# An early x tile in two loads, one z1 tile in other PSUM banks, and x tiles 2 to 4 taken transposed from DRAM

## The chip, the cores and the metric

One core of one Trainium2 chip runs the whole kernel. A core has TensorE (PE in the views; its weight loads are PEld), VectorE (DVE), ScalarE (ACT), GpSimd (POOL) and SyncE (SP), 16 DMA engines that serve queues issued from SP, ACT and POOL, an on-chip SBUF of 128 partitions, and eight PSUM banks that PE writes. The metric is the time of one execution in device microseconds, as the median of several runs.

## The reference, cut to what matters

All is float32: a sequence of 2048 rows of 512 features, 32 heads of 16.

```python
xn = layernorm(x)                                    # per row
# branch A: linear attention with a learned feature map
q, k, v = split(xn @ wqkv)                           # 32 heads of 16
pq, pk  = q @ w_phi, k @ w_phi                       # per head
phi(p)  = concat(softmax(p), softmax(-p))
o = phi(pq) (phi(pk)^T v) / (phi(pq) . sum(phi(pk)) + 1e-6)
# branch B: gated MLP that mixes along the sequence
z  = gelu(xn @ w_in);  z1, z2 = halves of z          # 688 columns each
g  = w_sp @ layernorm(z2) + b_sp                     # 2048 x 2048 mixing matrix
out = x + o @ wo + (z1 * g) @ w_out
```

## The kernel before

A float32 product is made of three products of rounded halves: each operand is split into a high part (`round_h`, mostly on ACT) and a rest (`rest_l`, mostly on DVE), and `mm3` (lines 51 to 55) adds high·high, high·low and low·high in PSUM. The 2048 rows are 16 tiles of 128 rows (`NT`). PE needs each x tile transposed, features on the partitions, and split: that is `xT[s]`.

The layernorm is never applied as such. A tile is centred (its row means taken away), and the reciprocal deviation `r_x[:, s]` is put on where a product leaves PSUM, as the `scale` of the activation. `stats` (line 251) makes mean and variance on DVE, `rstd_of` (line 84) two small POOL operations.

There are two ways from x in DRAM to `xT[s]`:

- **By PE.** The tile is loaded with rows on the partitions (`load_x`), centred on DVE (`centered_on_dve`, tiles 0, 1 and 3) or on ACT (`center`, tiles 2 and 4), and turned by four PE transposes into a PSUM bank (`transposed`, line 290). `split_x` (line 244) then reads the bank. Tiles 0 to 4 go this way (`XT0 = 5`).
- **By DMA.** `fetch_T` (line 265) loads a block of `x_t`, a copy of x that is transposed in 128 x 128 pieces ahead of the kernel, into a `raw` buffer (two of them). The same tile also comes with rows on the partitions, for its statistics alone. `mean_out` (line 271) puts the negated means into a padded 128 x 32 tile, turns that with a DVE transpose of 32 x 32 blocks, and stores the row to DRAM (`nm_d`) from SP's queue. `mean_in` (line 281) is an accumulating transfer on POOL's queue: it reads that row for all 128 partitions and adds it to `raw`. `split_x` then reads `raw` from SBUF. Tiles 5 to 15 go this way.

The first stage (`p0`, from line 175) runs so. The loads are issued in one written order (lines 340 to 351): x tile 0, the value weights (on ACT's and SP's queues in turn), x tile 1, the feature map `bd`, the key weights, x 2, the query weights, x 3, the first half of `w_in` (`w1r`, four pieces of 344 KB), x 4 and 5, the bias. Then a block (line 373 on) whose order is written out: `keep` makes everything issued later on an engine stay behind the instruction that it is given. It holds warm-up matmuls, tile 0's centring, transposes and value projection, tile 1, the folding of the feature map into the key weights (`fold`, 128 small matmuls, then `folded` which rounds the result), the value projection of tile 1, the key projection of tiles 0 and 1, and the folding of the query weights in two halves (the first half's last rounding on ACT is `q_half`).

After that comes the loop over the 16 tiles (line 427). Per tile: the key softmax pair on DVE and ACT (`softmax_k`), `split_x` of tile s+2, loads for tiles s+4 and s+5, `normalise` with an accumulation of 512 KB into `zacc` on POOL's queue, the value projection of tile s+1, mean transfers for tile s+4, query projections, z1 products (`z1_raw`: a zero to one tile per step, in PSUM pool `za`), and every second step `run`, which holds the PE order of transposes and the key-value products (`add_kv`). The four roundings of `w1r` on ACT and their rests on POOL (1.68 us each, to `w1_hl`) are traced in step 1 and stay behind `q_half`.

Within what the written order leaves open, a planner chooses each engine's order at compile time from its own cost estimates; `tc.issue_after(i)` puts a block's instructions behind `i` on `i`'s engine. An engine runs its own list in that fixed order and waits where an input or a buffer is not ready.

PSUM in this stage: `kv_ps` two banks, `za` two, `p0ps` four, of which the projections and the transposes take tag `mm`. When the stage ends, `p0ps` is given back, and `zb` (`zbp`, one tile of two banks) and `psk` (two) take its place. The last five z1 tiles (`LAG = 5`, s = 11 to 15) alternate: odd ones in `zbp`, even ones in `za` (line 578).

Later stages (z2, the mixing with `w_sp` in seven products per pair of tiles, the gate, the output) aren't touched.

Of the kernel before, what the change touches and what calls it, by code (L numbers as in the profile page):

```python
# [10 lines left out]
F32 = mybir.dt.float32  # L11
# [16 lines left out]
EPS_LN = 1e-5  # L28
EPS_DEN = 1e-6
XB = 3  # L30
XT0 = 5
NP = NT // 2
HP, QP = P // 2, P // 4
SQ = 32
# [3 lines left out]
def mixer(ctx: ExitStack, tc: tile.TileContext, x, x_t, wv, wqkT, phi_bd, wo, w_in, wst, b_r, w_out, out):  # L38
# [45 lines left out]
    def rstd_of(mv, r, stats=None):  # L84
        if stats is not None:
            dve.bn_aggr(mv, stats)
        pool.tensor_scalar_add(mv[:, 1:2], mv[:, 1:2], EPS_LN)
        pool.tensor_tensor(r, mv[:, 1:2], mhalf, op=ALU.pow)
# [83 lines left out]
    with ExitStack() as p0:  # L172
# [67 lines left out]
        def fetch(s):  # L240
            if s < NT:
                xt[s] = load_x(s)

        def split_x(src):
            t = xz.tile([P, 2, FH], F32R, tag="xz", name="xT")
            xT.append(t)
            src = src.rearrange("p a b -> p (a b)")
            return round_h(act, t[:, 0, :D], src), rest_l(t[:, 1, :D], src, t[:, 0, :D])
# [3 lines left out]
            dve.bn_stats(st6, xt[s])  # L252
            return dve.bn_aggr(mv_x[:, s], st6).ins

        def center(s):
            nm = wk.tile([P, 1], F32, tag="nm", name="nm")
            pool.tensor_scalar_mul(nm, mv_x[:, s, 0:1], -1.0)
            rstd_of(mv_x[:, s], r_x[:, s:s + 1])
            return act.activation(xt[s], xt[s], AF.Identity, bias=nm).ins

        raws = {}
        nm_pad = wk.tile([P, SQ], F32, tag="pad", bufs=1, name="nm_pad")
        pool.memset(nm_pad, 0.0)
# [1 line left out]
        def fetch_T(s):  # L265
            if s < NT:
                raws[s] = wk.tile([P, ND * P], F32, tag="raw", name="raw")
                sp.dma_start(raws[s], x_t[s].rearrange("p a b -> p (a b)"))
                fetch(s + 1)

        def mean_out(s):
            stats(s)
            xt.pop(s)
            dve.tensor_scalar_mul(nm_pad[:, :1], mv_x[:, s, 0:1], -1.0)
            row = wk.tile([P, SQ], F32, tag="nmT", bufs=1, name="nmT")
            dve.transpose(row, nm_pad)
            rstd_of(mv_x[:, s], r_x[:, s:s + 1])
            sp.dma_start(nm_d[s].rearrange("c (b t) -> b c t", t=SQ),
                         row.rearrange("(b k) t -> b k t", k=SQ)[:, 0].unsqueeze(1).to_broadcast([P // SQ, ND, SQ]))

        def mean_in(s):
            pool.dma_start(raws[s], nm_d[s:s + 1].rearrange("a c t -> a (c t)").to_broadcast([P, ND * P]), accum_op=ALU.add)

        def centered_on_dve(s):
            stats(s)
# [4 lines left out]
        def transposed(s):  # L290
            xs = xt.pop(s)
            pt = ps.tile([P, ND, P], F32, tag="mm", name="pt")
            for c in range(ND):
                ins = pe.transpose(pt[:, c], xs[:, c * P:(c + 1) * P], ident).ins
            return pt, ins
# [24 lines left out]
                                start=s == 0 and m < 4, stop=s == NT - 1, skip_group_check=True).ins  # L320
            return ins

        def run(tiles, feats):

            with ExitStack() as order:
                for i in ahead_of_run:
                    order.enter_context(tc.issue_after(i))
                ahead_of_run.clear()
                pts = []
                for t in tiles:  # L330
                    pt, i = transposed(t)
                    pts.append(pt)
                    order.enter_context(tc.issue_after(i))
                for t, e in feats:
                    i = add_kv(t, e)
            for pt in pts:
                split_x(pt)
            return i

        fetch(0)  # L340
        wvr = load_rows(wv, queues=(act, sp))
        fetch(1)
        sp.dma_start(bd, phi_bd.rearrange("p g f -> p (g f)"))
# [2 lines left out]
        wqT = load_rows(wqkT[:D])  # L346
        fetch(3)
        w1r = load_rows(w_in[:, :FH], FH)
        fetch(4)
        fetch(5)  # L350
        sp.dma_start(bias, b_r)


        def keep(**ins):
            for i in ins.values():
                queue.enter_context(tc.issue_after(i))
# [16 lines left out]
        with ExitStack() as queue:  # L373
            warm = wk.tile([P, 2 * P], F32, tag="v", bufs=4, name="warm")
            keep(dve=dve.memset(warm, 1.0).ins)
            tbl = wk.tile([P, 1], F32, tag="nm", name="tbl")
            keep(act=act.activation(tbl, mhalf, AF.Identity, bias=mhalf).ins)
            warm_up(4)
            keep(dve=centered_on_dve(0))
            split_v(0)  # L380
            split_v(1)
            pt, i = transposed(0)
            keep(pe=i)
            warm_up(1)
            split_x_kept(pt)
            split_v(2)
            split_v(3)
            keep(dve=centered_on_dve(1))
            keep(dve=stats(2))
            i, j = proj_v(0, True)  # L390
            keep(pe=i, act=j)
            pt, i = transposed(1)
            keep(pe=i)
            split_x_kept(pt)
            keep(act=center(2))
            accs = [fold_banks(pl, n) for n, pl in enumerate((za, kv_ps_p))]
            for g in range(NG):
                keep(pe=fold(wkT, g, accs))
            folded(1, accs, keep)
            kvps = kv_ps_p.tile([P, D], F32, tag="z", name="kvps")  # L400
            kv_acc = kvps[:, :NG * HP].rearrange("p (g b) -> p g b", b=HP)
            pt, i = transposed(2)
            keep(pe=i)
            split_x_kept(pt)
            keep(dve=centered_on_dve(3))
            keep(pe=proj_v(1)[0])
            p = proj(0, wqk_h[:, 1], wqk_l[:, 1], True)
            keep(pe=proj.last)
            pt, i = transposed(3)
            keep(pe=i)  # L410
            split_x(pt)
            ek = softmax_k(0, p)
            for k in range(2):
                accs = [fold_banks(za, k)]
                for g in range(NG):
                    i = fold(wqT, g, accs)
                q_parts = {}
                folded(0, accs, q_parts.update)
                if k == 0:
                    q_half = q_parts["act"]  # L420
                    keep(pe=i)
                    p1 = proj(1, wqk_h[:, 1], wqk_l[:, 1])
                    keep(pe=proj.last)
        n1 = nq = 0
        feats, shifted = [], softmax_pair.shifted
        behind = ExitStack()
        for s in range(NT):
            er = ek if s == 0 else softmax_k(s, p1 if s == 1 else proj(s, wqk_h[:, 1], wqk_l[:, 1]))
            ahead_of_run.append(proj.last)
            if XT0 <= s + 2 < NT:  # L430
                with tc.issue_after(softmax_pair.exp):
                    split_x(raws.pop(s + 2).rearrange("p (a b) -> p a b", b=P))
            if s:
                fetch_T(s + 4)
            feats.append((s, normalise(er)))
            if 0 < s < NT - 1:
                ahead_of_run.append(proj_v(s + 1)[0])
            if s == 1:
                with tc.issue_after(shifted):
                    stats(4)  # L440
                with tc.issue_after(q_half):
                    center(4)
            if 0 < s < NT - 4:
                with tc.issue_after(shifted):
                    mean_out(s + 4)
                with tc.issue_after(normalise.last):
                    mean_in(s + 4)
                shifted = softmax_pair.shifted
            while nq < (s - 2) * NT // (NT - 3):
                proj_q(nq)  # L450
                ahead_of_run.append(proj.last)
                nq += 1
            if s == 1:
                with tc.issue_after(q_half):
                    for c in range(ND):
                        round_h(act, w1_hl[0][:, c], w1r[c])
                        rest_l(w1_hl[1][:, c], w1r[c], w1_hl[0][:, c], pool)
            while n1 < (s + 1) * (NT - LAG) // (NT - 1):
                z1_raw(wk, za, n1, 2)
                n1 += 1  # L460
            if s and s % 2 == 0:
                last = run([t for t in (s + 2,) if t < XT0], feats[:-1])
                behind.close()
                behind.enter_context(tc.issue_after(last))
                del feats[:-1]
# [79 lines left out]
    with ExitStack() as p1:  # L545
# [27 lines left out]
        with ExitStack() as p1a:  # L573
            ta = p1a.enter_context(left("tmp1a", 1))
            for j in range(2):
                load_win(w2[j], 2 + j, ta)
            for s in range(NT - LAG, NT):
                z1_raw(tmp1, (za, zbp)[s % 2], s, 2)
                if s == NT - LAG + 1:
                    make_zb()  # L580
            make_kvT()
            raw[0], raw[1] = load_a(0), load_a(1)
            A[0] = prep_a(0, raw.pop(0))
# [406 lines left out]
```

## Time and profile before

| what | us |
|---|---|
| median of 3 runs (637.16 to 637.48) | 637.43 |
| the profiled execution | 638.0 |
| its span, first to last instruction | 636.3 |
| PE busy in it | 629.2 |
| DVE busy | 509.7 |
| ACT busy | 267.2 |
| POOL busy | 113.5 |

The granted TensorE clock is 0.999 of full over the span. The page gives busy time per engine over the whole span, so an engine that is nearly always busy in one stage can look half idle. The views used below are the page (whole span), waits (who waited for whom: total, times, longest), the timeline (start, duration, engine, line, operation, `x` the number merged, and in brackets the idle time before it with what ended it), groups by line or by tile, DMA issues with the time to landing, and busy time by window. A timeline row with a `q` behind the engine (`SPq`) is the issuing of a transfer, not the transfer.

### The profile page before, as it was taken

What the parts mean: (1) busy time and instruction counts of PE and PEld (TensorE: products, weight loads), DVE (VectorE), ACT (ScalarE), POOL (GpSimd) and SP (SyncE); (2) the same over time, 40 slices, a digit from 0 to 9 for tenths busy, and PEclk for the clock granted to TensorE, in tenths of its full rate; (3) what the DMA queues carried; (4) which work ended last, traced back from release to release, by engine and by line L of the source; (5) the groups of instructions that cost most, each with busy time, mean ns of one, the idle gap of its engine ahead of it and who ended that gap; (6) DMA issues with size and microseconds to landing.
All of it is one profiled execution on the core that took longest, in us unless ns stands there. A gap on an engine that the chain in (4) does not pass through costs nothing.

```text
span 636.3 us, 11626 instructions
## 1 busy us (share of the span) xinstructions
PE 629.2 (99%) x4467; PEld 571.2 (90%) x4467; DVE 509.7 (80%) x941; ACT 267.2 (42%) x446; POOL 113.5 (18%) x195
## 2 busy tenths in 40 slices
PE   8999999999999999999999999999999999999997
PEld 6888888888887999999999999999999887888886
DVE  5979989998898578889987868678695698989521
ACT  5623333332432448887443434434353433323330
POOL 4542231322101014341010010100101200001000
PEclk9999999999999999999999999999999999999999
DMA  9467676656644941002464352543548877675620
GB/s 329 142 165 162 192 183 148 192 142 155 182 136 112 309 141 66 2 1 73 140 191 126 117 170 87 176 131 113 179 151 265 274 269 271 246 266 218 210 67 35
DMA packets 41908, 103.95 MB, mean 163 GB/s; under 512 B 5404, under 2 KB 6940, under 8 KB 41852
## 3 DMA queue, kind: packets, MB, share of 16 engines
q1 hardware_dynamic: 28524, 58.37, 28.5%
q0 software_dynamic: 10736, 38.67, 21.2%
q10 hardware_dynamic: 2592, 6.16, 2.5%
q8 instruction: 35, 0.57, 0.4%
q14 instruction: 21, 0.17, 0.1%
HBM read 62.01 MB, written 26.50 MB: 139 GB/s over the span
## 4 chain that ended last, share of the span: by engine, by line
PE 94%; DVE 4%; issue 1%; DMA 1%; ACT 0%; POOL 0%
PE g L55 11%; PE g L54 11%; PE g L53 11%; PE proj L53 6%; PE proj L55 6%; PE proj L54 6%; PE zps L53 6%; PE zps L55 6%; PE zps L54 6%; PE pout L53 6%; PE pout L54 5%; PE pout L55 5%; PE ptq L863 1%; PE po L877 1%; PE pout L895 1%; PE kvps L319 1%
## 5 line engine op out<-in xcount | busy, mean ns | idle before, releaser
L54 PE MATMUL g<-B,A 128*128 128x344 f32 x448 | 143.3, 320 | 0.0
L55 PE MATMUL g<-B,A 128*128 128x344 f32 x448 | 143.3, 320 | 0.0
L53 PE MATMUL g<-B,A 128*128 128x344 f32 x448 | 143.3, 320 | 0.0
L54 PEld LDWEIGHTS g<-B,A 128*128 128x128 f32 x448 | 84.2, 188 | 0.0
L55 PEld LDWEIGHTS g<-B,A 128*128 128x128 f32 x448 | 84.2, 188 | 0.0
L53 PEld LDWEIGHTS g<-B,A 128*128 128x128 f32 x448 | 84.2, 188 | 0.0
L49 DVE TENSOR_TENSOR A<-S,A 128x512 fp32r<-128x512 f32 x64 | 43.7, 688 | 29.9 <-ACT A L45 29.1
L45 ACT ACTIVATE A<-S 128x512 fp32r<-128x512 f32 x64 | 40.1, 631 | 59.5 <-PE g L55 35.8
L113 ACT ACTIVATE e<-e,r_x 128x1024 f32<-128x1024 f32 x32 | 36.8, 1149 | 49.9 <-DVE e L112 48.0
L45 ACT ACTIVATE A<-wf 128x512 fp32r<-128x512 f32 x64 | 33.4, 522 | 39.8 <-PE g L55 34.5
L53 PE MATMUL proj<-wqk_h,xT 128*128 128x512 f32 x124 | 49.6, 400 | 0.0
L55 PE MATMUL proj<-wqk_h,xT 128*128 128x512 f32 x124 | 48.8, 394 | 0.0
L54 PE MATMUL proj<-wqk_l,xT 128*128 128x512 f32 x124 | 48.7, 393 | 0.0
L115 DVE TENSOR_REDUCE sm<-e 128x64 f32<-128x1024 f32 x32 | 38.6, 1211 | 8.8 <-ACT e L113 8.6
L53 PE MATMUL zps<-w_h,xT 128*128 128x344 f32 x128 | 41.8, 327 | 1.3 <-DVE e L112 0.9
L49 DVE TENSOR_TENSOR A<-wf,A 128x512 fp32r<-128x512 f32 x64 | 35.4, 553 | 8.4 <-ACT A L45 8.0
L55 PE MATMUL zps<-w_h,xT 128*128 128x344 f32 x128 | 40.9, 320 | 0.0
L54 PE MATMUL zps<-w_l,xT 128*128 128x344 f32 x128 | 40.8, 319 | 0.0
L731 POOL DMA_DIRECT2D u_d<-z1t x16 | 8.7, 547 | 133.0 <-DVE A L49 109.2
L53 PE MATMUL pout<-wu,uh 128*128 128x512 f32 (+1 forms) x80 | 31.6, 395 | 0.0
L54 PE MATMUL pout<-wu,uh 128*128 128x512 f32 (+1 forms) x80 | 30.4, 380 | 0.0
L55 PE MATMUL pout<-wu,ul 128*128 128x512 f32 (+1 forms) x80 | 30.4, 380 | 0.0
(203 smaller groups left out, 1470.5 us busy)
## 6 DMA issues: line engine op xcount, KB each, us to landing
wf<-in_wst SPq DMA_DIRECT2D x64, 256.0 KB, 3.4
e_d<-e POOLq DMA_DIRECT2D x16, 544.0 KB, 3.5
et<-e_d SPq DMA_DIRECT2D x16, 544.0 KB, 5.3
zacc<-e POOLq DMA_DIRECT2D x16, 512.0 KB, 4.9
er<-et POOLq DMA_DIRECT2D x12, 512.0 KB, 4.0
u_d<-z1t POOLq DMA_DIRECT2D x16, 368.0 KB, 4.6
u<-u_d SPq DMA_DIRECT2D x15, 368.0 KB, 3.0
z_d<-z1f ACTq DMA_DIRECT2D x16, 344.0 KB, 3.0
```

Source lines behind the costliest of these rows:

```text
L45: return act.activation(h, src, AF.Copy).ins
L49: return (eng or dve).tensor_tensor(l, src, h.bitcast(F32), op=ALU.subtract).ins
L53: pe.matmul(dst, ah, bh, start=start, stop=False)
L54: pe.matmul(dst, ah, bl, start=False, stop=False)
L55: return pe.matmul(dst, al, bh, start=False, stop=stop).ins
L113: softmax_pair.exp = act.activation(e, e, AF.Exp, scale=scale).ins
L115: dve.tensor_reduce(sm, heads(e), axis=AX.X, op=ALU.add)
L319: ins = pe.matmul(kv_acc[k:k + QP, m // 4], vs[:, m * QP:(m + 1) * QP], e[:, m * HP:(m + 1) * HP], start=s == 0 and m < 4, stop=s == NT - ...
L731: pool.dma_start(u_d[2 * i + k], z[:, k])
L863: pe.transpose(pt[:, a, k].bitcast(F32R), src, ident_r)
L877: lasts[3] = pe.matmul(po[r][c * QP:(c + 1) * QP, j // NG], kvT[rows, j], fs[j // 2][rows, j % 2], start=True, stop=True).ins
L895: pe.matmul(p, rt, w[:, ds], start=False, stop=False)
```

## The change

Three edits. The first x tile is loaded in two halves of 64 rows, one on SP's queue and one on ACT's, both ahead of the value weights. z1 tile 11 goes to `za` (with 12 and 14), and `zbp` keeps 13 and 15. And `XT0` becomes 2: tiles 2, 3 and 4 come by DMA as the later ones do. For tiles 2 and 3 the means are stored from POOL's queue, and both `mean_in` are issued behind the second store; their raw blocks are loaded behind `w1r`. The roundings of `w1r` move ahead of the loop: on ACT behind `q_half`, on POOL behind the issue of the last of the two `mean_in`; every `split_x` in the loop stays behind the last of these roundings on ACT. The loads, means and transfers of tile 4 start in step 0 of the loop. `center` goes, and `run` keeps only the key-value products.

```diff
-XT0 = 5
+XT0 = 2
...
                 raws[s] = wk.tile([P, ND * P], F32, tag="raw", name="raw")
                 sp.dma_start(raws[s], x_t[s].rearrange("p a b -> p (a b)"))
-                fetch(s + 1)
...
-        def mean_out(s):
+        def mean_out(s, queue=sp):
...
-        fetch(0)
+        xt[0] = wk.tile([P, D], F32, tag="x", bufs=XB, name="xt")
+        for k, queue in enumerate((sp, act)):
+            rows = slice(k * HP, (k + 1) * HP)
+            queue.dma_start(xt[0][rows], x[rows, :])
         wvr = load_rows(wv, queues=(act, sp))
...
         w1r = load_rows(w_in[:, :FH], FH)
+        fetch_T(2)
+        fetch_T(3)
         fetch(4)
-        fetch(5)
...
             keep(dve=centered_on_dve(1))
-            keep(dve=stats(2))
+            keep(dve=mean_out(2, pool))
...
-            keep(act=center(2))
...
-            pt, i = transposed(2)
-            keep(pe=i)
-            split_x_kept(pt)
-            keep(dve=centered_on_dve(3))
+            keep(dve=mean_out(3, pool))
+            with tc.issue_after(mean_out.stored):
+                mean_in(2)
+                mean_in(3)
             keep(pe=proj_v(1)[0])
             p = proj(0, wqk_h[:, 1], wqk_l[:, 1], True)
             keep(pe=proj.last)
-            pt, i = transposed(3)
-            keep(pe=i)
-            split_x(pt)
...
+        with tc.issue_after(q_half), tc.issue_after(mean_in.last):
+            for c in range(ND):
+                w1_half = round_h(act, w1_hl[0][:, c], w1r[c])
+                rest_l(w1_hl[1][:, c], w1r[c], w1_hl[0][:, c], pool)
...
             if XT0 <= s + 2 < NT:
-                with tc.issue_after(softmax_pair.exp):
+                with tc.issue_after(softmax_pair.exp), tc.issue_after(w1_half):
                     split_x(raws.pop(s + 2).rearrange("p (a b) -> p a b", b=P))
-            if s:
-                fetch_T(s + 4)
+            fetch_T(s + 4)
+            fetch(s + 5)
...
-            if 0 < s < NT - 4:
+            if s < NT - 4:
                 with tc.issue_after(shifted):
                     mean_out(s + 4)
...
-                last = run([t for t in (s + 2,) if t < XT0], feats[:-1])
+                last = run(feats[:-1])
...
             for s in range(NT - LAG, NT):
-                z1_raw(tmp1, (za, zbp)[s % 2], s, 2)
+                z1_raw(tmp1, zbp if s % 2 and s > NT - LAG else za, s, 2)
```

## What was expected before the run

> **What bounds the kernel now.** I read the page's busy line and its chain first, then the waits of PE alone, and only then the timeline around each edit.
>
> ```profile
> PE 629.2 (99%) x4467; PEld 571.2 (90%) x4467; DVE 509.7 (80%) x941; ACT 267.2 (42%) x446; POOL 113.5 (18%) x195
> ...
> PE 94%; DVE 4%; issue 1%; DMA 1%; ACT 0%; POOL 0%
> ```
>
> TensorE is the bound: busy 629.2 of a span of 636.3 us, and 94% of the chain that ended last. The waits of PE, all of them, are few:
>
> ```profile
> PE idle L362 <- DVE warm L375: 1.2, 1, 1.2
> PE pt L294 <- POOL mv_x L87: 1.0, 1, 1.0
> PE zps L53 <- DVE e L112: 0.9, 1, 0.9
> PE zps L53 <- ACT z1f L143: 0.3, 1, 0.3
> ```
>
> So an edit pays in three ways only: PE starts its real work sooner, PE runs fewer instructions, or one of these waits closes. It costs where PE gets a wait that it has not now. The rest of the span, some 590 us after the first stage, follows PE and only shifts.
>
> **Term 1: the first x tile in halves.** The timeline of the start:
>
> ```profile
> 0.80 0.38 SPq L179 DMA_DIRECT2D xt<-in_x  x1
> ...
> 4.42 0.69 DVE L252 BATCH_NORM_STATS2 st<-xt 128x6 f32<-128x512 f32 x1 [3.23 <-DMA xt<-in_x]
> ...
> 5.76 0.63 ACT L45 ACTIVATE wv_h<-wrow 128x512 fp32r<-128x512 f32 x1 [0.53 <-DMA wrow<-in_wv]
> ...
> 7.12 0.60 ACT L45 ACTIVATE xT<-pt 128x512 fp32r<-128x512 f32 x1 [0.73 <-PE pt L294]
> ...
> 7.77 3.19 PE L232 MATMUL proj<-wv_h,xT 128*128 128x512 f32 x8
> ...
> 10.80 1.09 PE L232 MATMUL proj<-wv_l,xT 128*128 128x512 f32 x4
> ```
>
> ```profile
> 3.00:4.00 1.00, 1.00 (x4) 0.72 (x4) 0.00 (x0) 0.29 (x1) 0.85 (x3) 1.00 1.01 381
> ```
>
> Tile 0 lands 3.6 us after its issue, and DVE, PE and ACT each wait for it in turn. By the second view (busy time by window; the last two columns are the DMA share and GB/s) the DMA engines are full from 3 us on, at 381 GB/s, because ACT's first weight piece runs beside the x tile. With both halves first in their queues that piece, 256 KB, comes behind: at most 256 KB / 381 GB/s = 0.65 us off the landing. From the other side the weights land up to as much later, and ACT rounds two of them (the second at 5.76) before it takes the transposed tile at 7.12; if they slip by more than the 0.7 us of slack there, 0.3 us is lost. PE's first eight matmuls take 0.38 us each (7.77 to 10.80) where the next four take 0.23 ((1.09 - 0.40) / 3, the last being 0.40 long); if that pace is set by the time and not by the data, an earlier start gains only part. I take 0.4, ends -0.3 and 0.65.
>
> The Trainium skill speaks against any gain here: "DMA: Bandwidth & Descriptors", section Rules for kernel authors, says that spreading DMAs over issuing engines doesn't help bandwidth, since they all run on the same engines. The full share in the row agrees; by that alone this term is 0 and the sum below is 1.4. What the row leaves is the order of the bytes, and that is what I count.
>
> **Term 2: twelve transposes.** Tiles 2, 3 and 4 lose `transposed`; PE's rows for the first and the last of them, with what follows:
>
> ```profile
> 14.28 0.66 PE L294 MATMUL pt<-ident,xt 128*128 128x128 f32 x4
> 14.69 0.48 PE L53 MATMUL proj<-wv_h,xT 128*128 128x512 f32 x1
> ```
>
> ```profile
> 42.96 0.60 PE L294 MATMUL pt<-ident,xt 128*128 128x128 f32 x4
> ...
> 43.48 1.10 PE L319 MATMUL kvps<-e,v 128*32 128x64 f32 x64
> ```
>
> From start to start they hold PE 0.41 and 0.52 us. Part of the later figure is PE's change of operand size before the small attention products, which stays, so I take 0.42 for each of the three: 1.27 us in all, at most 3 x 0.52.
>
> **Term 3: other banks for one z1 tile.** The 0.9 us wait of PE:
>
> ```profile
> 203.85 0.32 PE L54 MATMUL zps<-w_l,xT 128*128 128x344 f32 x1
> ...
> 204.00 0.32 PE L55 MATMUL zps<-w_h,xT 128*128 128x344 f32 x1
> ...
> 205.01 0.68 DVE L112 TENSOR_TENSOR e<-mm,proj 128x512 f32<-128x512 f32 x1
> ...
> 205.77 1.15 ACT L113 ACTIVATE e<-e,r_x 128x1024 f32<-128x1024 f32 x1 [3.95 <-DVE e L112]
> ...
> 205.83 0.40 PE L53 MATMUL zps<-w_h,xT 128*128 128x344 f32 x1 [0.93 <-DVE e L112]
> ```
>
> Tile 11 needs the banks that the last query softmax still reads. In `za` it has no such wait: 0.93 us. But then tile 12, also in `za`, waits until ACT has emptied tile 11. If ACT's order puts that behind the exponential of 205.77, PE goes on at 205.77 + 1.15 + 0.54 = 207.5 (0.54 us is one evacuation, the `z1f` row below) and 1.6 us are lost instead. ACT idles 3.95 us before it, time for both evacuations, so I take the gain.
>
> ```profile
> L143 ACT ACTIVATE z1f<-zps,r_x 128x344 f32<-128x344 f32 x4 | 2.2, 544 | 3.3 <-PE zps L55 2.9 <-ACT z1f L143 0.4
> ```
>
> **Term 4: the wait for tile 2.** Now PE, ACT, DVE and POOL around 20 us:
>
> ```profile
> 17.80 0.68 DVE L252 BATCH_NORM_STATS2 st<-xt 128x6 f32<-128x512 f32 x1
> ...
> 22.06 1.09 ACT L45 ACTIVATE wqk_h<-fold 128x512 fp32r<-128x512 f32 x2 [0.51 <-PE fold L209]
> ...
> 23.04 1.45 ACT L45 ACTIVATE w_h<-wrow 128x688 fp32r<-128x688 f32 x2
> ...
> 23.89 1.68 POOL L49 TENSOR_TENSOR w_l<-wrow,w_h 128x688 fp32r<-128x688 f32 x1 [3.96 <-ACT w_h L45]
> ...
> 24.37 1.15 ACT L113 ACTIVATE e<-e,r_x 128x1024 f32<-128x1024 f32 x1
> ...
> 24.59 0.19 PEld L53 LDWEIGHTS proj<-wv_h,xT 128*128 128x128 f32 x1
> ...
> 28.63 1.16 PE L209 MATMUL fold<-bd,wrow 64*64 64x64 f32 x64
> ```
>
> Before, PE takes tile 2 at 24.6, transposed long since. After, its split waits on ACT for four roundings of `w1` and the first exponential. Fold q0 ends 0.4 + 0.41 + 0.43 us earlier, at 20.8; ACT then has 1.09 + 2 x 1.45 + 1.15 = 5.1 us in hand, so tile 2's high half is there at 20.8 + 5.1 + 0.6 = 26.5. PE ends the key projection of tile 1 at 23.3 (24.6 less 1.24) and has the second query fold, 1.1 us: idle from 24.4, **at most 2.1 us**. The nearest filler is z1 of tile 0. POOL, done with issuing `mean_in(3)` at about 22.5 (below), gives a piece of `w1_l` every 1.68 us; the first two, at 24.2 and 25.9, free six matmuls each of 0.15 us (203.85 to 204.00), of which 1.0 to 1.6 us fit before 26.5. That PE's written order mixes products, the trace shows where a value projection is followed by a key projection before it is complete:
>
> ```profile
> 47.64 0.39 PE L54 MATMUL proj<-wv_l,xT 128*128 128x512 f32 x1
> ...
> 47.86 0.39 PE L53 MATMUL proj<-wqk_h,xT 128*128 128x512 f32 x1
> ```
>
> I take 0.8 us left, ends 0 and 2.1.
>
> The transfers must come in time for that.
>
> ```profile
> 19.37 0.56 POOL L88 TENSOR_TENSOR r_x<-mv_x,mhalf 128x1 f32<-128x1 f32 x1
> ...
> 40.34 0.21 DVE L276 STREAM_TRANSPOSE nmT<-nm_pad 128x32 f32<-128x32 f32 x1
> ...
> 46.06 1.24 POOL L282 DMA_DIRECT2D raw<-nm_d  x1
> ```
>
> Statistics of tile 3 start at 17.1 instead of 17.8 (one split of 0.68 no longer lies ahead); with 0.68 of their own, the pad and the 0.21 transpose the row is there at 18.3. POOL, after two operations of some 0.56, issues the store until about 19.6, then `mean_in(2)` and, when its own row is stored, `mean_in(3)`, 1.24 each: 22.5 with some wait.
>
> ```profile
> raw<-nm_d POOLq DMA_DIRECT2D x11, 256.0 KB, 6.3
> ...
> DMA to landing us min/median/max: 4.9/6.3/7.7
> ```
>
> At the median of 6.3 us from issue to landing it lands at 25.9, just before ACT is free; the eleven each run behind a 512 KB accumulation, which this one doesn't. Their ends, 4.9 and 7.7, give 24.5 and 27.3.
>
> **Edits at nothing.** DVE gains a pad copy and the 0.21 transpose for each of three tiles, some 0.35 us, and loses a centring; ACT loses two centrings. DMA gains three loads and three accumulations of 256 KB.
>
> ```profile
> 20.00:30.00 10.00, 10.00 (x164) 8.05 (x163) 9.48 (x19) 6.97 (x11) 5.95 (x7) 1.00 0.24 65
> 30.00:40.00 10.00, 9.88 (x53) 8.66 (x53) 9.97 (x17) 3.75 (x6) 5.80 (x8) 1.00 0.37 82
> ```
>
> DMA shares of 0.24 and 0.37 hide the transfers. DVE, 9.97 of 10, hides nothing, but its chain starts with PE's key projection, 1.2 us sooner; without that, 0.35 us for tile 4. On SP, the load of tile 4's block waits for tile 2's split (27), with tile 4's mean store behind it; PE wants tile 4 only at 44. The 0.3 us wait on ACT I leave as it is.
>
> **The sum**: 0.4 + 1.27 + 0.93 - 0.8 = 1.8 us. The profiled execution took 638.0 us (span 636.3), 0.6 above the median of the runs; the difference carries over: 637.43 - 1.8 = **635.6 us**.
>
> **Rivals.**
> - *The wait isn't filled* (2.1 for 0.8): 636.9. For it: POOL's `w1_l` pieces stand behind two accumulating transfers. Chance 0.20.
> - *The transfer ends last: slower.* If `mean_in(2)` takes the 7.7 us, and ACT and DVE another 1.3, tile 2 is whole at 28.6; with no filler PE idles 4.2 us and then restarts at the pace of its start, eight matmuls at 0.38 for 0.23, 1.2 us: 2.6 gained, 5.4 lost, 640.2. It decides from a wait of 2.6 us on. Against it: no 512 KB transfer ahead. The Trainium skill, "TensorE: Matmul & The Clock Gate", Part 1, has the clock halved after an idle window of 3.4 us and for as long of new work; by it the restart is an estimated 1.7 us, 640.7. Chance 0.10.
> - *The z1 tile turns round* (term 3 at -1.6): 638.2. Chance 0.08.
> - *The halves do nothing*, the second queue starting later: 636.0. Chance 0.10.
> - *More than the sum*: no wait at all, 0.65 at the start, and the eight slow matmuls at full pace (1.2): 4.0 us, 633.4. Chance 0.07.
>
> **How the numbers follow.** The forecast keeps 0.45, with a range of its own from 634.9 to 636.3. Under 0.2% (1.3 us) a measurement can't tell this kernel's time from no change. Faster by more: 0.42 of the forecast, 0.08 of the halves' case, 0.07 of the last: 0.57. Slower by more: 0.10. The rest, 0.33, is the same. From 634.4 to 638.4 all but the slow transfer and the largest gain are in, 0.83.
>
> **What would show it.** Right: DVE's first statistics near 4.0; no `pt` after tile 1; no wait of PE on DVE's L112 at 204; PE idle around 24 to 26.5 for under a microsecond, `zps` ahead of the value projection of tile 2. Wrong: PE waiting there for a split whose ACT waited on the DMA of `raw`; matmuls 0.4 us apart after it; a wait of `zps` on `z1f` after 200.

## The result, and where the time went

| | before | after |
|---|---|---|
| median us (runs) | 637.45 (4, 637.16 to 637.88) | 644.51 (4, 643.99 to 645.96) |
| ratio, 95% interval | | 1.0113 (1.01 to 1.0126) |
| profiled execution, its span | 638.0, 636.3 | 644.44, 642.7 |
| PE busy in the span | 629.2 | 632.2 |
| mean granted TensorE clock | 0.999 | 0.989 |

The change makes the kernel 7.1 us **slower**; 635.6 was forecast. All waits of PE in the changed kernel (us in total, times, longest):

```profile
PE proj L232 <- ACT xT L45: 1.8, 1, 1.8
PE proj L55 <- DVE xT L49: 1.5, 1, 1.5
PE proj L53 <- ACT xT L45: 1.3, 2, 1.0
PE idle L353 <- DVE warm L366: 1.2, 1, 1.2
PE fold L209 <- DVE wqk_l L49: 0.8, 1, 0.8
PE pt L288 <- POOL mv_x L87: 0.6, 1, 0.6
```

The 0.9 us wait of z1 at 204 us is gone, as meant. New are four kinds of wait: one for tile 0 at the start (L232), and three on tiles 2 and 3 and the query weights. The timeline of PE shows the last three (start, duration; in brackets the idle time before):

```profile
25.10 1.15 PE L209 MATMUL fold<-bd,wrow 64*64 64x64 f32 x32
27.08 1.15 PE L209 MATMUL fold<-bd,wrow 64*64 64x64 f32 x32 [0.83 <-DVE wqk_l L49]
28.53 0.80 PE L53 MATMUL proj<-wv_h,xT 128*128 128x512 f32 x1 [0.30 <-ACT xT L45]
29.12 0.63 PE L54 MATMUL proj<-wv_l,xT 128*128 128x512 f32 x1
...
31.57 0.79 PE L53 MATMUL proj<-wv_h,xT 128*128 128x512 f32 x1 [0.97 <-ACT xT L45]
32.16 0.63 PE L54 MATMUL proj<-wv_l,xT 128*128 128x512 f32 x1
34.33 0.79 PE L55 MATMUL proj<-wv_h,xT 128*128 128x512 f32 x1 [1.54 <-DVE xT L49]
...
51.03 1.10 PE L313 MATMUL kvps<-e,v 128*32 128x64 f32 x64
```

The first key-value product starts at 51.03 where it started at 43.48, with the same products ahead of it: 7.55 us are lost by then. The four waits are 0.83 + 0.30 + 0.97 + 1.54 = 3.6 us. The rest is pace: from 28.53 on a projection matmul of 512 columns starts 0.43 us after the one before (29.55 after 29.12), where it was 0.23 in the kernel before. Sixteen go like that up to 38.7 and take 4.0 us more than at 0.23. The start is 1.0 late, and the two transposed tiles that are left out ahead of 20 us (tiles 2 and 3) and the third later give back 1.27. Behind 51 us about 1.1 us come back, most of it from the z1 edit.

The pace is the clock. Busy time by stretches of 3.4 us of the changed kernel, cut where the clock changes (columns: window, length, PE, PEld, DVE, ACT, POOL busy, granted clock, DMA share, GB/s):

```profile
25.10:28.50 3.40, 2.30 (x65) 2.02 (x64) 3.39 (x6) 3.40 (x7) 3.32 (x5) 1.00 0.71 155
28.50:31.90 3.40, 2.41 (x5) 1.50 (x6) 3.40 (x6) 2.61 (x4) 3.40 (x3) 0.50 0.14 29
31.90:35.30 3.40, 1.86 (x4) 1.00 (x4) 3.40 (x4) 0.00 (x0) 2.70 (x2) 0.50 0.46 145
35.30:38.70 3.40, 3.40 (x9) 2.64 (x8) 3.40 (x9) 0.00 (x0) 1.45 (x4) 0.50 0.92 209
38.70:42.10 3.40, 3.40 (x18) 2.91 (x17) 1.30 (x4) 0.69 (x1) 0.41 (x1) 1.00 0.27 88
```

Here a stretch in which PE is busy 2.30 of 3.40 us is followed by half the clock, and the full clock comes back behind the first stretch in which PE is busy throughout. Waiting is paid for twice. Busy time alone gives no clean limit: in the kernel with tiles 2 to 4 by DMA alone (below), two stretches with 2.18 and 2.36 us busy (from 21.73 and 25.14 on) are followed by the full clock, and one with 0.72 (from 28.56 on) by half.

Who makes tile 2 late? ACT, DVE and POOL of the changed kernel:

```profile
25.19 2.76 ACT L45 ACTIVATE w_h<-wrow 128x688 fp32r<-128x688 f32 x4
...
27.86 0.62 ACT L45 ACTIVATE xT<-raw 128x512 fp32r<-128x512 f32 x1
```

```profile
29.14 0.67 DVE L112 TENSOR_TENSOR e<-mm,proj 128x512 f32<-128x512 f32 x1
29.73 1.28 DVE L252 BATCH_NORM_STATS2 st<-xt 128x6 f32<-128x512 f32 x2
30.93 1.30 DVE L305 TENSOR_TENSOR e<-e 128x1024 f32<-128x1024 f32 x1
32.15 2.12 DVE L49 TENSOR_TENSOR xT<-raw,xT 128x512 fp32r<-128x512 f32 x1
34.20 1.27 DVE L49 TENSOR_TENSOR wqk_l<-fold,wqk_h 128x512 fp32r<-128x512 f32 x2
```

```profile
26.28 7.45 POOL L49 TENSOR_TENSOR w_l<-wrow,w_h 128x688 fp32r<-128x688 f32 x4
```

ACT takes tile 2's high half right behind the four roundings of `w1`, with no idle time before it: the transferred data lay there (issued at 21.62, landed at 25.66). DVE could take the rest at 28.5; in the order that the planner gave DVE it stands behind the second softmax's subtractions, two statistics and the first normalisation, and runs at 32.15. Then it takes 2.12 us, beside POOL's `w_l`. PE's third product of tile 2 needs it: 34.33.

From this I formed theory A (tiles 2 and 3 by DMA are the cost: orders on ACT and DVE, then the clock) against theory B (the start, 1 us late and at half clock, sets it off), and tried the parts alone.

### The profile page after: what moved, and what is told of

Same layout as the page of the kernel before. It is cut to its first block, busy times and chain, and to the rows that moved or that the text cites. A ratio compares the mean times of both kernels' runs of the same rounds, so it can differ in the third digit from the quotient of the medians.

```text
span 642.7 us, 11629 instructions
## 1 busy us (share of the span) xinstructions
PE 632.2 (98%) x4455; PEld 572.5 (89%) x4455; DVE 510.1 (79%) x946; ACT 266.9 (42%) x445; POOL 117.0 (18%) x198
## 4 chain that ended last, share of the span: by engine, by line
PE 96%; DVE 2%; DMA 1%; issue 0%; ACT 0%; ACTq 0%
PE g L53 11%; PE g L54 11%; PE g L55 11%; PE proj L53 7%; PE proj L55 7%; PE proj L54 6%; PE zps L53 6%; PE zps L55 6%; PE zps L54 6%; PE pout L53 6%; PE pout L54 5%; PE pout L55 5%; PE ptq L846 1%; PE po L860 1%; PE kvps L313 1%; PE pout L878 1%
## 5 line engine op out<-in xcount | busy, mean ns | idle before, releaser
L143 ACT ACTIVATE z1f<-zps,r_x 128x344 f32<-128x344 f32 (+1 forms) x30 | 17.0, 565 | 36.7 <-PE zps L55 36.6
L293 ACT ACTIVATE v<-proj,r_x 128x512 f32<-128x512 f32 x16 | 11.0, 685 | 50.0 <-PE proj L55 46.8
L53 PE MATMUL pout<-wu,uh 128*128 128x512 f32 (+1 forms) x80 | 31.6, 395 | 0.0
```

The source lines that it names most:

```text
L53: pe.matmul(dst, ah, bh, start=start, stop=False)
L143: z1_raw.last = act.activation(z[:, k], p, AF.Copy, scale=r_x[:, s:s + 1]).ins
L293: ins = act.activation(v[s], proj(s, wv_h, wv_l, rest_last), AF.Copy, scale=r_x[:, s:s + 1]).ins
```

## The experiments

Each run has its own runs of the kernel before beside it (medians 637.1 to 637.3).

| kernel | us, median (runs) | ratio to before, 95% |
|---|---|---|
| first x tile in halves only | 639.58 (5) | 1.0035 (1.0023 to 1.0048) |
| both halves on SP's queue | 639.95 (5) | 1.0046 (1.0033 to 1.0059) |
| z1 tile 11 in `za` only | 637.46 (11) | 0.9998 (0.999 to 1.0007) |
| tiles 2 to 4 by DMA only | 644.68 (4) | 1.0112 (1.0096 to 1.0127) |
| tile 4 by DMA only | 637.42 (11) | 1.0004 (0.9995 to 1.0013) |
| tiles 3 and 4 by DMA | 641.81 (5) | 1.0076 (1.0064 to 1.0089) |
| the same, split of tile 3 early | 643.22 (4) | 1.0087 (1.0074 to 1.01) |
| change, split of tile 2 early | 639.48 (10) | 1.0036 (1.0017 to 1.0055) |
| change, transfers early | 645.13 (4) | 1.014 (1.0118 to 1.0161) |
| change, both | 639.22 (4) | 1.0035 (1.0021 to 1.0049) |
| both, first tile whole | 636.84 (11) | 0.9993 (0.9984 to 1.0002) |
| the last, DVE's rest put back | 640.11 (6) | 1.0046 (1.003 to 1.0062) |
| change, rests of `w1` later | 648.44 (4) | 1.0173 (1.0158 to 1.0189) |
| change, PE filled | 653.27 (4) | 1.025 (1.0236 to 1.0264) |

### The parts of the change alone

The kernel before with the first tile's two loads:

```diff
-        fetch(0)
+        xt[0] = wk.tile([P, D], F32, tag="x", bufs=XB, name="xt")
+        for k, queue in enumerate((sp, act)):
+            rows = slice(k * HP, (k + 1) * HP)
+            queue.dma_start(xt[0][rows], x[rows, :])
```

> The kernel before with the first x tile in two halves and nothing else. Theory A (tiles 2 and 3 by DMA cost the time, the start adds its 1.0 us): 637.45 + 1.0 = 638.5, DVE's first statistics near 3.95 us, ACT's second rounding of wv near 6.6 instead of 5.8, the fold near 13.3 instead of 12.25. Theory B (the late start is what sets off the slow clock and the waits further on): over 641, with the slow matmuls of 28 to 38 us here too. My prediction on record had 637.0 for this edit.

The kernel before with line 578's `(za, zbp)[s % 2]` as in the change:

> The kernel before with z1 tile 11 in za and nothing else. Both theories: the wait of 0.93 us of PE on DVE's subtraction at 204 us goes, 637.45 - 0.9 = 636.5. If the gain is taken back by a later wait, 637.4; if tile 12 then waits for ACT, 638 or more.

The changed kernel with the two other edits undone:

> The changed kernel without its other two edits: the first x tile in one load, z1 tile 11 in zb again, tiles 2 to 4 by DMA. Theory A: the waits and slow matmuls between 28 and 38 us are all there, 644.5 - 1.0 + 0.9 = 644.4, with the chain of 20 to 28 us at most 1 us earlier. Theory B: without the late start tile 2 comes nearly in time, the slow matmuls go, and twelve transposes are saved: 637.45 - 1.27 + 0.8 = 637.0, at most 639.

The kernel before with tile 4 alone by DMA:

```diff
-XT0 = 5
+XT0 = 4
...
-        fetch(5)
...
-            if s:
-                fetch_T(s + 4)
+            fetch_T(s + 4)
...
-            if s == 1:
-                with tc.issue_after(shifted):
-                    stats(4)
-                with tc.issue_after(q_half):
-                    center(4)
-            if 0 < s < NT - 4:
+            if s < NT - 4:
```

> The kernel before with tile 4 alone taken by DMA (tiles 2 and 3 by PE as before). Theory A: tile 4 is wanted only at 44 us, its transfer is hidden, and four transposes go: 637.45 - 0.4 = 637.0; no matmul of 0.4 us between 28 and 38. If what costs the time is the transfers and mean stores as such (a third theory, C: DMA and DVE work of the new tiles slows this stage), 638.5 or more.

Theory A holds: the tiles alone cost 7.4 us, as much as all three edits. In their profile PE reaches the first query fold 2.4 us earlier than in the changed kernel (18.62 for 21.04), and the first key-value product only 0.6 earlier (50.47 for 51.03): the late tile absorbs the start. So the costs don't add up. Tile 4 alone changes nothing that can be measured. Its profile shows where the gain from the four transposes goes: ACT's split of tile 4 now stands ahead of an evacuation of z1, and PE's wait for that is 0.9 us where it was 0.3.

The halves cost 2.2 us by themselves, more than the 1.0 of theory A; the slow matmuls of theory B, between 28 and 38 us, aren't in their profile, and its 641 isn't reached. The z1 edit gives nothing by itself. Its profile shows where the gain goes: the wait at 204 is closed, and the later products (`g`) now wait for DVE.

```profile
PE g L53 <- DVE c L713: 0.5, 1, 0.5
```

From the first to the last of these products it takes 213.29 us, 212.22 in the kernel before. In the changed kernel it takes 212.18, so there the gain is kept. Why the same edit ends in one case in a wait of DVE and not in the other I didn't try; the planner's orders of that stage differ. The tiles alone, with the old banks for z1, take 213.08 us there, so the longer stretch isn't tied to this edit.

### Why the halves cost

```diff
-        for k, queue in enumerate((sp, act)):
+        for k, queue in enumerate((sp, sp)):
```

> The kernel before with the first x tile in two halves, but both on SP's queue, so that ACT's queue begins with value weights as before. Theory: the halves alone cost 2.2 us because the half on ACT's queue puts the value weights 1 us later (ACT's second rounding of wv at 6.4 for 5.2 to 5.8): here it is back at 5.2 to 5.8, and the time at 637.3 within 0.6. Rival: two transfers instead of one cost by themselves (more descriptors, a later landing): 638.5 or more.

The rival holds. DVE's first statistics (which wait for x), ACT's second rounding of `wv` and PE's first eight projection matmuls, with one half on each queue (the quickest of its five runs was profiled) and then with both on SP's:

```profile
3.99 0.69 DVE L252 BATCH_NORM_STATS2 st<-xt 128x6 f32<-128x512 f32 x1 [2.80 <-DMA xt<-in_x]
...
6.43 0.63 ACT L45 ACTIVATE wv_h<-wrow 128x512 fp32r<-128x512 f32 x1 [1.25 <-DMA wrow<-in_wv]
...
7.60 2.47 PE L232 MATMUL proj<-wv_h,xT 128*128 128x512 f32 x8
```

```profile
5.83 0.70 DVE L252 BATCH_NORM_STATS2 st<-xt 128x6 f32<-128x512 f32 x1 [4.65 <-DMA xt<-in_x]
6.43 0.63 ACT L45 ACTIVATE wv_h<-wrow 128x512 fp32r<-128x512 f32 x1 [2.17 <-DMA wrow<-in_wv]
...
9.13 3.78 PE L232 MATMUL proj<-wv_h,xT 128*128 128x512 f32 x8
```

With the whole tile, in profiles whose start is the same code, the statistics began at 4.42 (before), 4.29 (tile 4 only), 3.96 (tiles 2 to 4) and 3.84 (z1 only), and the second rounding at 5.76, 5.57, 5.30 and 5.20. So on two queues x lands no earlier than in the better half of these, and the weights 0.7 to 1.2 us later; on one queue both are late. The DMA engines move less: from 3 to 5 us 305 and 322 GB/s with two queues, 301 and 250 with one, where the kernel before has 381 and 395, with the engines as fully busy (shares of 0.92 to 1.07). In all eight profiles with halves the rate there is 197 to 322 GB/s, in all eight with the whole tile 361 to 412. Why halves of 64 rows move slower stays open. The rule of the Trainium skill that the prediction cited ("DMA: Bandwidth & Descriptors", Rules for kernel authors: more issuing engines give no more bandwidth) is borne out (two queues move no more than the one load did), and the runs show a loss beyond it.

The clock adds to it. A trace records the granted clock from some point of the start on; ahead of that the views print 1.00. Up to that point projection matmuls start 0.43 us apart, behind it 0.23 (in the kernel before the record begins at 10.12, and matmuls start at 9.64, 10.07, 10.34, 10.57). In the eight profiles with the whole tile the record begins between 4.1 and 10.5 us, the clock stays full through the start, and the first fold starts between 10.8 and 12.3. In the eight with halves it begins between 4.4 and 13.3, in three of them half the clock is granted again behind PE's wait for tile 0 (in the changed kernel from 8.00 to 11.41), and the fold starts between 11.6 and 15.0. The profile with one half on each queue is one of the better ones: its fold starts at 11.64, ahead of the 12.25 of the kernel before, and its first key-value product at 43.55 for 43.48, so the 2.2 us can't be read from it. Its eight matmuls above take 2.47 us, behind a record that begins at 7.4; with both halves on SP's queue they take 3.78, ahead of one that begins at 13.3. Of the other four runs with one half on each queue three have a mean clock of 0.996 or 0.997; no run of the kernel before is under 0.999. How much of the 2.2 us is the later data and how much the clock, no run separates.

### ACT's order or the transfers

The split of tile 2 ahead of the roundings of `w1`:

```diff
-        with tc.issue_after(q_half), tc.issue_after(mean_in.last):
+        with tc.issue_after(q_half):
+            high, rest = split_x(raws.pop(2).rearrange("p (a b) -> p a b", b=P))
+        with tc.issue_after(high), tc.issue_after(mean_in.last):
             for c in range(ND):
...
-            if XT0 <= s + 2 < NT:
+            if XT0 < s + 2 < NT:
```

> The changed kernel with the split of tile 2 on ACT ahead of the four roundings of w1 (behind the first half of the query weights), the rest unchanged. Theory A1 (ACT's order delays tile 2: the split's high half stands behind four roundings of 0.7 us, and the planner then puts DVE's rest behind the second softmax): the high half is done at 26.4 us instead of 28.5, when the transfer of the means has landed, the rest near 27 instead of 34.3; the two waits of 1.3 and 1.5 us on tile 2 and 3 and most of the slow matmuls go, first kvps near 45 instead of 51: 644.5 - 6 = 638.5. Theory A2 (the chain of transfers, nm_d to raw, ends last): at most 1 us better, 643.5.

The transfers earlier (row buffer of tile 3 in another slot, so that it doesn't wait for the store of tile 2):

```diff
-            row = wk.tile([P, SQ], F32, tag="nmT", bufs=1, name="nmT")
+            row = wk.tile([P, SQ], F32, tag="zf" if s == 3 else "nmT", bufs=2 if s == 3 else 1, name="nmT")
...
+        fetch_T(2)
+        fetch_T(3)
         w1r = load_rows(w_in[:, :FH], FH)
-        fetch_T(2)
-        fetch_T(3)
...
             keep(dve=mean_out(2, pool))
+            with tc.issue_after(mean_out.stored):
+                mean_in(2)
...
             with tc.issue_after(mean_out.stored):
-                mean_in(2)
                 mean_in(3)
```

> The changed kernel with the transfers earlier: transposed blocks of tiles 2 and 3 loaded ahead of w1, the means of tile 2 added right behind their store and not behind that of tile 3, a second buffer for the row of means. ACT's order as in the changed kernel. Theory A1 (ACT's order ends last): raw is whole 1 to 2 us earlier and nobody takes it, 644.5 within 0.7. Theory A2 (the transfers end last): 642.5 or less.

> Both edits: the split of tile 2 ahead of the roundings of w1, and the transfers earlier. Theory A1: now the transfers are what ends last for tile 2, so another 1 us over the first edit alone, 637.5, near the kernel before. Theory A2: as the transfers alone, 642.5 or less. If both are wrong and the accumulating transfers themselves cost the time, over 643.

Theory A1 holds: the order gives 5.0 us, the transfers alone nothing. (With this edit the planner also puts four projections of tile 2 ahead of PE's second query fold; the 5.0 us are the edit with what follows from it.) With them early, ACT still takes tile 2 right behind the roundings (first fence), and DVE takes 2.12 us for the rest. With the split early, both are where they should be (second fence), and none of the 3.4 us stretches from 21 to 34.6 us has less than the full clock.

```profile
23.89 2.76 ACT L45 ACTIVATE w_h<-wrow 128x688 fp32r<-128x688 f32 x4
26.55 0.62 ACT L45 ACTIVATE xT<-raw 128x512 fp32r<-128x512 f32 x1
...
30.96 2.12 DVE L49 TENSOR_TENSOR xT<-raw,xT 128x512 fp32r<-128x512 f32 x1
```

```profile
26.92 0.63 ACT L45 ACTIVATE xT<-raw 128x512 fp32r<-128x512 f32 x1 [0.71 <-DMA raw<-nm_d]
...
27.86 0.68 DVE L49 TENSOR_TENSOR xT<-raw,xT 128x512 fp32r<-128x512 f32 x1
```

Both together don't give the further microsecond that A1 had. Their runs spread widely (636.91 to 643.55 with the split early), as with the halves; the three longest with the split early (641.4 to 643.55) have a mean clock of 0.994, the others 0.997 to 1.0.

### The start put back, and DVE's order alone

Both repairs with `fetch(0)` as before:

> The changed kernel with both repairs of tile 2 (its split ahead of the roundings of w1, its transfers earlier) and the first x tile in one load again. Theory A: the start is 1 to 2.5 us earlier (fold near 11.1 instead of 13.9), but tile 2's transfers land at a time of their own, so part of it is waited away: 637.0, no better than the kernel before by more than 0.5. If the start carries over in full: 636.2. If the halves were harmless beside the rest: 639.

636.84 against 637.21, within what can be told apart. So the loss is explained by undoing: 644.51 to 639.22 by ACT's and DVE's order together with the earlier transfers (5.3 us), to 636.84 by the whole first tile (2.4), and what is left of the change is worth 0.4 (by the interval, from 1.0 gained to 0.1 lost). Its waits show why it isn't 1.27 + 0.93: tile 2 still ends 0.5 us late, and the later products wait 0.9.

```profile
PE g L55 <- DVE A L49: 0.6, 2, 0.4
PE proj L53 <- ACT xT L45: 0.5, 1, 0.5
PE g L53 <- DVE c L696: 0.3, 1, 0.3
```

In this kernel I put DVE's rest back behind the second softmax, and nothing else; PE's order in this stage is unchanged, and on DVE the planner moves one of the rests of the query weights as well, behind the first normalisation:

```diff
-            high, rest = split_x(raws.pop(2).rearrange("p (a b) -> p a b", b=P))
+            x2 = raws.pop(2)
+            t2 = xz.tile([P, 2, FH], F32R, tag="xz", name="xT")
+            xT.append(t2)
+            high = round_h(act, t2[:, 0, :D], x2)
...
+            if s == 1:
+                with tc.issue_after(softmax_pair.shifted):
+                    rest_l(t2[:, 1, :D], x2, t2[:, 0, :D])
             if XT0 < s + 2 < NT:
```

> The last kernel (both repairs of tile 2, first x tile whole, 636.84) with DVE's rest of tile 2 put back behind the subtractions of the second softmax; ACT's high half stays early, PE's order stays the same. Theory A1 in its sharper form (DVE's order costs as much as ACT's: PE's third product of tile 2 needs the rest): the rest comes near 28.5 instead of 25.5, PE waits 2 to 3 us for it and starts again at 0.43 us a matmul: 639 to 641. Rival (ACT's order alone was the cause, DVE's followed from it and costs nothing by itself): 637 within 0.7.

It costs 3.3 us. One DVE instruction of 0.75 us moved from 24.87 to 28.08; PE waits 1.6 us for it, and the clock follows: half of it for 3.4 us, which is 1.7 us of work (windows of this kernel):

```profile
28.08 0.75 DVE L49 TENSOR_TENSOR xT<-raw,xT 128x512 fp32r<-128x512 f32 x1
```

```profile
25.40:28.80 3.40, 1.93 (x36) 1.39 (x34) 3.40 (x7) 3.40 (x7) 3.32 (x5) 1.00 0.45 77
28.80:32.20 3.40, 3.31 (x8) 2.64 (x9) 3.40 (x6) 1.40 (x2) 3.40 (x2) 0.52 0.51 154
32.20:35.60 3.40, 3.40 (x16) 2.78 (x15) 3.21 (x7) 0.69 (x1) 3.40 (x4) 0.98 0.30 84
```

### The pace, and the rest beside POOL

38 products whose results are thrown away, 9 ahead of the second query fold and 29 behind it; the projections of tile 2 come behind them:

> The changed kernel with 38 warm-up products (128x256, results thrown away) on PE: nine between the key projection of tile 1 and the second query fold, 29 behind that fold, where PE idles between 25 and 34 us; the projections of tile 2 come behind them. Theory A (the slow matmuls between 28 and 38 us come from PE's idle stretches): the products take 0.21 us each, the projections behind them go at 0.23 us from the first one on and not at 0.43; since the fill delays the few matmuls that ran between the waits, the time gains little, 644.5 - 0.6 = 643.9. Rival (the slow pace comes from other engines' work beside PE): the projections still go at 0.43, and the time is 646 or more.

Each piece took 0.43 us, in two matmuls, not 0.21, so the fill lasted twice as long as meant and the time says nothing. The pace does: with PE kept busy the clock stays full from 25 to 45 us, beside 7.92 us of POOL's work and 9.93 of DVE's in the first 10 us, and the projections behind the fill go at 0.23 us from the second one on. So it isn't the other engines' work.

```profile
25.00:35.00 10.00, 10.00 (x106) 8.48 (x105) 9.93 (x16) 7.45 (x11) 7.92 (x7) 1.00 0.42 99
35.00:45.00 10.00, 10.00 (x48) 8.78 (x47) 6.08 (x14) 0.00 (x0) 5.25 (x8) 1.00 0.85 185
```

The rests of `w1` on POOL moved behind the first accumulation:

```diff
                 w1_half = round_h(act, w1_hl[0][:, c], w1r[c])
-                rest_l(w1_hl[1][:, c], w1r[c], w1_hl[0][:, c], pool)
...
             feats.append((s, normalise(er)))
+            if s == 0:
+                with tc.issue_after(normalise.last):
+                    for c in range(ND):
+                        rest_l(w1_hl[1][:, c], w1r[c], w1_hl[0][:, c], pool)
```

> The changed kernel with the four rests of w1 on POOL behind the first accumulation into zacc instead of ahead of it. Theory (beside POOL's tensor operations DVE's rest of tile 2, SBUF to SBUF, takes 2.12 us instead of 0.68): it takes 0.68, PE's second wait is 1.4 us shorter: 643.1, or 644 if z1 of tile 0 then waits for w_l. Rival (the 2.12 us are a wait for the data of the transfer): still 2.1 us, no gain.

```profile
33.66 0.68 DVE L49 TENSOR_TENSOR xT<-raw,xT 128x512 fp32r<-128x512 f32 x1
...
34.94 6.85 POOL L49 TENSOR_TENSOR w_l<-wrow,w_h 128x688 fp32r<-128x688 f32 x4
...
36.72 5.64 DVE L49 TENSOR_TENSOR xT<-raw,xT 128x512 fp32r<-128x512 f32 x1
```

The theory holds for the mechanism: with POOL idle tile 2's rest takes 0.68 us. But the block only moves. Tile 3's rest now falls into POOL's four operations and takes 5.64 us, the third softmax is late behind it, z1 waits 3.1 us, and the kernel is 3.9 us slower than the changed one.

### Tiles 3 and 4: the order, or the transfer

The kernel before with tiles 3 and 4 by DMA (`XT0 = 3`; `mean_out(3, pool)` and `mean_in(3)` where tile 3 was centred, its block loaded behind `w1r`):

> The kernel before with tiles 3 and 4 by DMA, tile 2 by PE as before. Theory A (it is tile 2's way that is too long, from load to split): eight transposes go, tile 3 has some 4 us more than tile 2 had and comes nearly in time: 637.2 - 0.84 = 636.4, and if tile 3 is 1 us late 637.4. If one tile by DMA ahead of w1's roundings is enough to start the trouble: 640 or more.

4.6 us slower, against what I expected: tile 2 was not alone. Tile 3's split stood behind the second exponential on ACT (32.22) and its rest at 34.73 on DVE. So I moved the split behind `q_half`, as for tile 2:

```diff
+        with tc.issue_after(q_half):
+            high, rest = split_x(raws.pop(3).rearrange("p (a b) -> p a b", b=P))
         n1 = nq = 0
...
-            if XT0 <= s + 2 < NT:
+            if XT0 < s + 2 < NT:
```

> The kernel with tiles 3 and 4 by DMA (641.81), but tile 3's split behind the first half of the query weights on ACT instead of behind the second exponential. Theory (order, not transfer: tile 3's data lay ready while its split stood behind the exponential on ACT and behind the first normalisation on DVE): the waits of 1.1 and 2.0 us and the slow matmuls behind them go, 637.2 - 0.84 = 636.4, up to 637.2 if ACT now waits for the transfer with other work behind it. Rival (the transfers and their traffic cost the time): 640 or more.

```profile
24.13 0.58 ACT L45 ACTIVATE wqk_h<-fold 128x512 fp32r<-128x512 f32 x1
29.29 0.63 ACT L45 ACTIVATE xT<-raw 128x512 fp32r<-128x512 f32 x1 [4.58 <-DMA raw<-nm_d]
29.83 2.77 ACT L45 ACTIVATE w_h<-wrow 128x688 fp32r<-128x688 f32 x4
...
30.67 7.50 POOL L49 TENSOR_TENSOR w_l<-wrow,w_h 128x688 fp32r<-128x688 f32 x4 [3.39 <-ACT w_h L45]
...
37.88 0.68 DVE L49 TENSOR_TENSOR wqk_l<-fold,wqk_h 128x512 fp32r<-128x512 f32 x1
...
38.61 0.66 PE L53 MATMUL zps<-w_h,xT 128*128 128x344 f32 x1 [4.12 <-DVE nm_pad L274]
```

Neither theory as it stood. The waits on tile 3 are gone, but the time isn't: tile 3's means start for DRAM only at 19.64 and its block is whole at 29.3, ACT waits 4.58 us for it with the roundings of `w1` behind, and PE waits 4.1 us at z1 instead. The row puts that down to DVE's small `nm_pad`, but by the times it is DVE's rest of the query weights just before it: z1 takes the two banks of `za` that the second query fold held, and the first of them is free when this rest ends, at 37.88 + 0.68 = 38.56. The rest stands behind the second softmax and the first normalisation, which were late behind tile 3. POOL's `w_l`, which z1 needs too, ended at 38.2, hardly earlier. For tile 3, then, the transfer is late as well, and PE has nothing else in this stretch: with the split first, what follows it on ACT, DVE and POOL is late; with the roundings first, the split is. For tile 2, whose means leave at 13.35, ACT waits only 0.8 us when the split goes first (in the kernel of 636.84).

## Why the prediction was wrong, step by step

- **Term 4 is the step that failed**, and in it "the nearest filler is z1 of tile 0": 0.8 us were taken, at most 2.1. Measured are 3.6 us of waits and 4.0 us of half clock. (1) The wait was ended with tile 2's *high half*; PE's third product needs the rest, and I never put that into DVE's order. That alone is worth 3.3 us (one instruction put back). (2) The high half came at 28.5, not 26.5: the start was 1.4 us behind my sum, and ACT idled 0.81 for DVE's subtraction, where I added its durations without a gap. (3) Nothing filled the wait, and z1 could not have: it takes the two banks of `za` that the second query fold holds until DVE's rests of it, 34.20 to 35.47. PE's order also has the projections of tiles 2 and 3 ahead of z1, and `w_l` is whole only at 33.7. (The 24.6 from which the idle time was reckoned is the start of a weight load; PE's own row is 24.83.)
- **The pace** of the restart was seen, but only in a rival and at 1.2 us, tied to an idle time of 4.2 us. Two short waits in one stretch set it off, and two more kept it for three. The Trainium skill, "TensorE: Matmul & The Clock Gate", Part 1, gives the window as 3.4 us and has the clock fall after an idle one; the lengths agree (28.5 to 38.7 is three of them), but here a window with PE busy 2.30 of 3.40 us was enough.
- **Term 1** has the wrong sign: 0.4 us gained was forecast (ends -0.3 and 0.65), 2.2 lost by itself. The step that failed is "at most 256 KB / 381 GB/s": it kept the rate and only reordered the bytes, and the rate fell (the quotient itself is 0.69, not 0.65). The first matmuls' pace is set by the time, which the prediction left open: it changes where the record of the clock begins. And 4.42, the landing to be improved on, was the latest of four.
- **Term 2** is right for tiles 2 and 3: the query fold starts at 20.85 + 1.02 - 0.83 = 21.04, the start being 1.02 late and two transposed tiles 0.83. The 0.42 of tile 4 didn't show by itself (637.42 for 637.27).
- **Term 3** is right for the wait, and its counter-case (z1 turning round) didn't come. That the gain can be given back 100 us later wasn't among the cases.
- **The rival "the transfer ends last"** gave 640.2: the right side, the wrong reason. The transfer was issued at 21.62, landed at 25.66, near the 25.9 of the prediction, and ACT never waited for it. Its sign that "would show it wrong" (a split whose ACT waited on `raw`) isn't in the trace; the matmuls 0.4 us apart are.

## What to carry to other kernels

When an operand changes its way, place every instruction of the new way, the last one above all, in the fixed order of each engine that runs it, and see what is queued ahead; durations added up without the waits between them are a lower bound. Count on a filler only when its PSUM banks are free. Short waits of TensorE close together cost twice where its clock follows its load: look at busy time in stretches of a few microseconds and not at the longest wait. And a landing time from one profile is one draw: look at several before planning to beat it.

## What the runs showed of the hardware that was not expected

- A VectorE operation with both inputs in SBUF that starts beside GpSimd's tensor operations can lose to several of them in a row: 5.64 us for 0.68, until POOL's fourth was done. An operation that takes one of its two inputs from PSUM wasn't held (`wqk_l<-fold` at 26.34 in the changed kernel, 0.68 us beside the same POOL work). The Trainium skill, "SBUF — State Buffer", Who interferes with whom, has the later one blocked until the other finishes; that fits the 2.12 us, and the 5.64 show it repeated.
- At the start the first value projections run at 0.43 us a matmul while the row of the clock reads 1.00 (before, 8 to 10 us); in another profile of the same code they go mostly at 0.23 (z1 only, 2.46 us for eight). The trace's record of the clock begins at 10.12 us in the first and at 6.44, ahead of these matmuls, in the second. Where it has no record the row reads 1.00, and the mean clock of 0.999 leaves that stretch out too; the distance between starts shows the slow pace.
- Two loads of 64 rows move fewer bytes than one of 128: 197 to 322 GB/s from 3 to 5 us for 361 to 412 (above).
